# Attention and a mixture of experts in one kernel: where the leftover batch's first transposes stand in TensorE's order

## The chip, the cores and the metric

The kernel runs on one core of a Trainium2 chip. The core has TensorE (PE in the profile; its weight loads are listed as PEld), VectorE (DVE), ScalarE (ACT), GpSimd (POOL) and SyncE (SP), which issues DMA transfers, as GpSimd does too. The metric is the device time of one execution in microseconds (us), as the median of five runs.

## What is computed

Multi-query attention (8 batches, 16 heads, 384 tokens, head size 64, one key and value head) gives 3072 token vectors of 1024 values. Each token then chooses one of 4 groups and one of the group's 4 experts, and goes through that expert's two matrices:

```python
scores = scale * np.matmul(q, k.transpose(0, 1, 3, 2))
attn = softmax(scores)
x = np.matmul(attn, v)                # (batch, head, token, 64) -> (3072, 1024)
g_idx = np.argmax(x @ w_group, axis=1)
e_idx = np.argmax(xg @ w_expert[g], axis=1)
h = np.maximum(xg[mask_e] @ w1[g, e], 0.0)
ye = h @ w2[g, e]
out[tok_idx] = combined[:, None] * ye     # combined: product of the two gate weights
```

(`softmax` stands for the usual lines, and `xg` for the tokens of group `g`.)

## The kernel before

**Stages.** The loop over `p` (24 blocks of 128 tokens, three for each batch) does the attention. For each finished batch the kernel finds the expert that most of its tokens chose, loads that expert's two matrices and runs the whole batch through them. Tokens that chose another expert are rare: one pair of batch and expert is taken as the "leftover" and computed apart at the end of the kernel, for up to 32 tokens gathered from its batch. A general, slow branch (`rare_block`) stands behind that for all other cases.

**Units.** A batch's pass through its expert is cut into 14 units of PE work by `moe_units`: eight `h_unit`s (called h0 to h7 below), each of 8 matmuls (L407) into one PSUM tile `hps`, which ScalarE evicts into `hT` (L408); and six `y_unit`s (y00, y01, y10, y11, y20, y21: block of 128 tokens, half of the columns), each of 8 matmuls (L417) into `yps`, which ScalarE scales and evicts into a row tile `y` (L419); when both halves of a block are there, SP stores it (L447). `fill(n)` emits the next n units. The order of instructions on each engine is that of the program text; no scheduler moves them. So the calls of `fill` decide which PE work stands between the steps of a longer chain.

**PSUM.** All side results (`hps`, `yps`, `pb`, `px`, `ph` and others) take turns on one ring of three buffers (`ps_s`, tag "s"). A tile can be written only when the tile three places before it in the program's order has been read out.

**The end of the kernel**, in the order of the text, from the last block's attention on:

- `weigh(NP - 1)` (L656) finishes batch 7's tokens; GpSimd casts them to bf16 (L301), and SP writes them to DRAM as `x_bf` (L303).
- L659: SP reads the leftover batch's tokens, `xe`, back from `x_bf`. The batch is known only at run time, so this read waits for that write.
- `fill(2)`, the gates of batch 7, `fill(3)`, the ranks of the leftover's tokens (L675 to L689), `fill(1)`, `counts`, `fill(1)`, the matmuls `pg` (L697, L698). With these, batch 6's last units and h0 to h3 of batch 7 have run.
- L710: `fill(3)` emits h4, h5 and h6.
- L712 to L719: for each of the three token blocks, 8 transposes of `xe` on PE into one PSUM tile `pb` (L715; pb0, pb1, pb2 below), VectorE's copy to `xt` (L717), and `fill(1)`: h7 behind pb0, y00 behind pb1, y01 behind pb2.
- L723: 24 matmuls `px` gather the chosen tokens out of the three `xt`; VectorE copies them to `xc` (L725).
- Then the leftover's expert: `ph` (L732) with its first matrix, `phT` (L738), `py` (L746) with its second, and `yc` (L748), each with a unit behind it (y10, y11, y20). The second matrix is loaded by `leftover_w2` (L582), which `fill` calls when batch 6's last unit is out. GpSimd scatters `yc` into `out` (L750), `spread` (L458 to L469) adds it to batch 7's last block, and the last stores go out (L466, L445).

Of the kernel before, what the change touches and what calls it, by code (L numbers as in the profile page):

```python
# [21 lines left out]
def kernel(  # L22
# [53 lines left out]
    def side(shape, dtype, name):  # L76
        return ps_s.tile(shape, dtype, tag="s", name=name)
# [351 lines left out]
    def first_units(b):  # L429
        rows = {}  # L430

        def place(st, cs):
            if cs.start == 0:
                rows[st] = pool.tile([P, Dm], FP32, tag="y", bufs=3, name="y")
            return rows[st][:, cs]

        def closes(st):
            return b == B - 1 and st == ST - 1

        def store(st, cs, y):  # L440
            if closes(st):
                if cs.start == 0:
                    leftover["row"] = y
                else:
                    nc.sync.dma_start(out=outv[b, :, st, cs], in_=y)  # L445
            elif cs.stop == Dm:
                nc.sync.dma_start(out=outv[b, :, st, :], in_=rows[st][:])  # L447

        def merge(st, cs, ps, y):
            if not closes(st) or cs.start == 0:  # L450
                return False
            if cs.start == CW:
                spread()
            nc.vector.scalar_tensor_tensor(out=y, in0=ps[:], scalar=gsel[b][:, st:st + 1], in1=leftover["y"][:, cs.start - CW:cs.stop - CW], op0=OP.mult, op1=OP.add)
            return True
        return moe_units(wts[b][0], wts[b][1], xbf[b], lambda: gsel[b], place, store, merge, lambda st, nh: 2 if closes(st) and nh == 1 else 1)
# [26 lines left out]
    def fill(n):  # L483
        while n > 0:
            if not units:
                if begun[0] >= B or begun[0] not in wts:
                    return
                units.extend(first_units(begun[0]))
                begun[0] += 1
            units.pop(0)()  # L490
            n -= 1
            ran[0] += 1
            if ran[0] == (FO + 2 * ST) * (B - 2) + FO:
                leftover_w1()
            if ran[0] == (FO + 2 * ST) * (B - 1):
                leftover_w2()
# [77 lines left out]
    def leftover_w1():  # L574
        leftover["e"], leftover["b"] = parts_of(leftover["reg"])
        w1 = wpool.tile([P, KO, F], BF16, tag="w1", name="w1")
        load_w1(w1, leftover["e"])
        leftover["w1"] = w1

    def leftover_w2():  # L580
        w2 = wpool.tile([P, FO, Dm], BF16, tag="w2", name="w2")
        nc.gpsimd.dma_start(out=w2[:], in_=w2f[bass.ds(leftover["e"], 1)].rearrange("a p k f -> (a p) k f"))  # L582
        leftover["w2"] = w2
    for p in range(NP):
        b, st = divmod(p, ST)
# [121 lines left out]
    nc.vector.tensor_sub(out=small[:, 1:2], in0=nfl[:], in1=small[:, 0:1])  # L707
    nex = pool.tile([1, 1], I32, tag="nex", bufs=1, name="nex")
    nc.vector.tensor_copy(out=nex[:], in_=small[0:1, 1:2])
    fill(3)  # L710
    xtok = []
    for st in range(ST):  # L712
        pb = side([P, Dm], BF16, "pb")
        for ko in range(KO):
            nc.tensor.transpose(out=pb[:, ko * P:(ko + 1) * P], in_=xe[:, ko, st * P:(st + 1) * P], identity=ident_bf[:])  # L715
        xt = pool.tile([P, Dm], BF16, tag="pt", bufs=9, name="xt")
        nc.vector.tensor_copy(out=xt[:], in_=pb[:])  # L717
        xtok.append(xt)
        fill(1)  # L719
    px = side([P, KO, CAP], FP32, "px")  # L720
    for ko in range(KO):
        for st in range(ST):
# [183 lines left out]
```

## Time and profile before

| what | value |
|---|---|
| median of five runs | 461.11 us (460.64 to 461.69) |
| the profiled execution | 460.88 us |
| its span in the profile | 459.4 us |
| PE clock granted | 0.995 of full speed |
| matmuls of the attention's scores, L251 | 1152, 142.7 us |
| matmuls of the attention's values, L290 | 1152, 141.1 us |
| matmuls of the h units, L407 | 512 shown, 86.7 us |
| matmuls of the y units, L417 | 380 shown, 85.0 us |
| transposes of `xe`, L715, from the first to the last start | 435.4 to 439.7 us |
| read of `xe`, issue to landing | 7.2 us |

All views are of one execution. Times in them count from the start of the span. A row of a timeline gives the start, the busy time, the engine, the line, the operation with its output and input tiles, the number of instructions, and in brackets the engine's idle time before the group with what ended it. A matmul's duration includes its way through the array, in which the next matmul already runs; distances between starts tell what a group costs. Some records of matmuls are missing in a trace (7 of 8 shown in some groups).

### The profile page before, as it was taken

What the parts mean: (1) busy time and instruction counts of PE and PEld (TensorE: products, weight loads), DVE (VectorE), ACT (ScalarE), POOL (GpSimd) and SP (SyncE); (2) the same over time, 40 slices, a digit from 0 to 9 for tenths busy, and PEclk for the clock granted to TensorE, in tenths of its full rate; (3) what the DMA queues carried; (4) which work ended last, traced back from release to release, by engine and by line L of the source; (5) the groups of instructions that cost most, each with busy time, mean ns of one, the idle gap of its engine ahead of it and who ended that gap; (6) DMA issues with size and microseconds to landing.
All of it is one profiled execution on the core that took longest, in us unless ns stands there. A gap on an engine that the chain in (4) does not pass through costs nothing.

```text
span 459.4 us, 10188 instructions
## 1 busy us (share of the span) xinstructions
PE 448.7 (98%) x4196; PEld 199.8 (43%) x4208; DVE 308.3 (67%) x488; ACT 241.9 (53%) x345; POOL 60.4 (13%) x83
## 2 busy tenths in 40 slices
PE   8999999999999999999999999999999999999893
PEld 6343445333643345433553335433464335434552
DVE  3899965499717996099843997269960999674421
ACT  2966643676337753576346763376535764541331
POOL 1004003000120113000030001200130000500000
PEclk9999999999999999999999999999999999999998
DMA  8787997996699395992969747994859920799982
GB/s 159 94 147 111 217 213 114 258 201 140 106 182 254 70 189 96 232 227 74 172 97 262 147 117 126 170 257 79 171 98 228 235 70 17 117 211 236 275 220 105
DMA packets 152454, 74.55 MB, mean 162 GB/s; under 512 B 120256, under 2 KB 138944, under 8 KB 152400
## 3 DMA queue, kind: packets, MB, share of 16 engines
q0 software_dynamic: 28416, 37.81, 48.4%
q1 hardware_dynamic: 122656, 35.68, 33.3%
q8 instruction: 35, 0.57, 0.5%
q10 hardware_dynamic: 1328, 0.33, 0.4%
q14 instruction: 19, 0.16, 0.1%
HBM read 92.62 MB, written 19.01 MB: 243 GB/s over the span
## 4 chain that ended last, share of the span: by engine, by line
PE 90%; DMA 3%; issue 3%; DVE 1%; POOL 0%; ACT 0%; SPq 0%; POOLq 0%; ACTq 0%
PE s L251 28%; PE o L290 25%; PE hps L407 16%; PE yps L417 16%; PE gps L312 2%; DMA x_bf<-xbf 2%; DMA xe<-x_bf 2%; PE qps L228 1%; PE warm L152 1%; POOL xbf L301 0%; DVE presum L261 0%; PE sm L273 0%; PE pb L715 0%; DVE rinv L280 0%; DVE xT L300 0%
## 5 line engine op out<-in xcount | busy, mean ns | idle before, releaser
L253 ACT ACTIVATE pt<-s 128x1024 f32<-128x1024 f32 x144 | 142.1, 1026 | 72.4 <-PE s L251 71.6
L251 PE MATMUL s<-qT,kT 64*64 64x512 f32 x1152 | 142.7, 594 | 0.0
L290 PE MATMUL o<-pt,v 64*64 64x512 f32 x1152 | 141.1, 590 | 0.0
L261 DVE TENSOR_TENSOR presum<-presum,pt 128x1024 f32<-128x1024 f32 x96 | 116.6, 1215 | 15.2 <-ACT pt L253 9.8
L407 PE MATMUL hps<-xbf,w 128*128 128x384 bf16 x512 | 86.7, 326 | 0.0
L417 PE MATMUL yps<-w,hT 128*128 128x512 bf16 (+1 forms) x380 | 85.0, 375 | 0.6
L259 DVE TENSOR_TENSOR presum<-pt 128x1024 f32<-128x1024 f32 x24 | 29.4, 1223 | 76.8 <-ACT pt L253 75.4
L290 PEld LDWEIGHTS o<-pt,v 64*64 64x64 f32 x1152 | 43.4, 133 | 76.8 <-issue 73.0
L251 PEld LDWEIGHTS s<-qT,kT 64*64 64x64 f32 x1152 | 40.8, 133 | 66.8 <-issue 60.2
L301 POOL CAST xbf<-xT 128x1024 bf16<-128x1024 f32 x24 | 25.0, 1041 | 302.9 <-DVE xT L300 302.9
L407 PEld LDWEIGHTS <-w 128*128 128x128 bf16 x512 | 48.1, 98 | 37.6 <-issue 6.5
L419 ACT ACTIVATE y<-yps,gsel 128x512 f32<-128x512 f32 x47 | 32.3, 687 | 58.8 <-PE yps L417 57.2
L408 ACT ACTIVATE hT<-hps 128x384 bf16<-128x384 f32 x64 | 31.2, 488 | 52.1 <-PE hps L407 48.0
L417 PEld LDWEIGHTS <-hT 128*128 128x128 bf16 x392 | 37.5, 98 | 44.2 <-issue 2.4
L145 POOL DMA_DIRECT2D w<-in_moe_w_dram x36 | 24.8, 707 | 58.1 <-DVE gsel L395 45.0
L300 DVE TENSOR_TENSOR xT<-o,rinv 128x1024 f32<-128x1024 f32 x24 | 29.1, 1214 | 2.5 <-PE o L290 2.5
L280 DVE STREAM_TRANSPOSE rinv<-rc 128x1024 f32<-128x1024 f32 x24 | 29.9, 1246 | 0.8
L265 DVE TRANSPOSE_TENSOR_REDUCE fold<-presum 128x32 f32<-128x1024 f32 x24 | 29.6, 1231 | 0.0
L243 DVE STREAM_TRANSPOSE qT<-qraw 128x1024 f32<-128x1024 f32 x20 | 23.6, 1202 | 0.0
L209 ACT ACTIVATE qraw<-qraw 128x1024 f32<-128x1024 f32 x21 | 22.0, 1048 | 0.0
L273 PEld LDWEIGHTS sm<-fold,sel 64*64 64x64 f32 x192 | 7.3, 133 | 13.3 <-issue 13.3
L371 ACT ACTIVATE ex<-dl 128x60 f32<-128x60 f32 x8 | 2.0, 253 | 20.1 <-DVE dl L369 20.1
(152 smaller groups left out, 161.9 us busy)
## 6 DMA issues: line engine op xcount, KB each, us to landing
w<-in_moe_w_dram POOLq DMA_DIRECT2D x36, 512.0 KB, 11.4
w<-in_moe_w_dram POOLq DMA_DIRECT2D x9, 2048.0 KB, 26.0
out_dram<-y SPq DMA_DIRECT2D x23, 512.0 KB, 7.3
qraw<-in_q_dram SPq DMA_DIRECT2D x56, 192.0 KB, 3.7
x_bf<-xbf SPq DMA_DIRECT2D x8, 768.0 KB, 3.9
v<-in_v_dram SPq DMA_DIRECT2D x16, 96.0 KB, 3.2
k<-in_k_dram SPq DMA_DIRECT2D x28, 48.0 KB, 2.6
qn<-in_q_dram SPq DMA_DIRECT2D x4, 256.0 KB, 5.2
```

Of the source, the lines that this page charges most:

```text
L251: nc.tensor.matmul(out=ps[64 * c:64 * c + 64, a, :], lhsT=kT[b][r, j * D:(j + 1) * D], rhs=qT[p][r, c * CW:(c + 1) * CW], start=True, stop ...
L253: nc.scalar.activation(out=t[:], in_=ps[:], func=ACTF.Exp, scale=scale)
L259: nc.vector.tensor_add(out=presum[p][:], in0=pt[p, 0][:], in1=pt[p, 1][:])
L261: nc.vector.tensor_add(out=presum[p][:], in0=presum[p][:], in1=pt[p, j][:])
L265: nc.vector.tensor_reduce(out=fold[p][:], in_=presum[p][:].rearrange("p a (n i) -> p (a n) i", i=32), axis=AX, op=OP.add, apply_transpose= ...
L280: nc.vector.transpose(out=t[:].rearrange("p (b i) -> p b i", i=32), in_=rc[:].rearrange("p c b -> p (c b)").unsqueeze(2).to_broadcast([P, ...
L290: nc.tensor.matmul(out=o_ps[p][64 * a:64 * a + 64, c, :], lhsT=v_sb[b][r, j, :], rhs=pt[p, j][r, a, :], start=(j == 0), stop=(j == KB - 1))
L300: nc.vector.tensor_mul(out=xT[b][:, :, ts], in0=o_ps[p][:].rearrange("p c (h n) -> p (c h) n", n=P), in1=rinv[p][:].rearrange("p (h n) -> ...
L407: nc.tensor.matmul(out=ps[:, 0:S], lhsT=w1[:, ko, fc * P:(fc + 1) * P], rhs=xb[:, ko, :], start=(ko == 0), stop=(ko == KO - 1))
L408: nc.scalar.activation(out=state["h"][:, fc, :], in_=ps[:, 0:S], func=ACTF.Relu)
L417: nc.tensor.matmul(out=ps[:], lhsT=state["h"][:, fo, st * P:(st + 1) * P], rhs=w2[:, fo, cs], start=(fo == 0), stop=(fo == FO - 1))
L419: nc.scalar.activation(out=y, in_=ps[:], func=ACTF.Copy, scale=gs_of()[:, st:st + 1])
```

## The change

```diff
     nc.vector.tensor_copy(out=nex[:], in_=small[0:1, 1:2])
-    fill(3)
+    fill(4)
     xtok = []
     for st in range(ST):
         pb = side([P, Dm], BF16, "pb")
...
         xt = pool.tile([P, Dm], BF16, tag="pt", bufs=9, name="xt")
         nc.vector.tensor_copy(out=xt[:], in_=pb[:])
         xtok.append(xt)
-        fill(1)
+        if st > 0:
+            fill(1)
```

`fill(4)` now emits h4 to h7 ahead of the first transposes, and no unit follows pb0. PE's order around it goes from h6, pb0, h7, pb1, y00, pb2, y01, px to h6, h7, pb0, pb1, y00, pb2, y01, px. The ring of three PSUM buffers is taken in the same new order. The other engines keep their order, and every instruction is still there.

## The prediction

> **What bounds the kernel now.** I read the page first: which engine is full, and what the chain of work that ended last is made of.
>
> ```profile
> span 459.4 us, 10188 instructions
> PE 448.7 (98%) x4196; PEld 199.8 (43%) x4208; DVE 308.3 (67%) x488; ACT 241.9 (53%) x345; POOL 60.4 (13%) x83
> ...
> PE 90%; DMA 3%; issue 3%; DVE 1%; POOL 0%; ACT 0%; SPq 0%; POOLq 0%; ACTq 0%
> ```
>
> TensorE (PE) is busy 98% of the span and makes 90% of the chain; DMA makes 3%, so there is little to win except where PE stands still. Next I read the chain in order of time from 420 us on, where the diff lies:
>
> ```profile
> 420.33 7.66 DMA x_bf<-xbf
> ...
> 428.11 7.21 DMA xe<-x_bf
> 435.32 0.05 issue
> 435.37 0.62 PE pb L715 x8
> 435.99 1.30 PE hps L407 x8
> 437.29 0.45 PE pb L715 x8
> ```
>
> Columns: start, duration, what. The chain leaves PE here: batch 7's tokens are written to DRAM (7.66 us), the leftover batch's tokens are read back from it (7.21 us, landing at 435.32), and only then do the first transposes start. From there to the end the chain is PE. What PE did meanwhile is in its timeline (start, busy, what, idle before it):
>
> ```profile
> 432.72 1.46 PE L407 MATMUL hps<-xbf,w 128*128 128x384 bf16 x8
> 435.37 0.62 PE L715 MATMUL pb<-ident_bf,xe 128*128 128x128 bf16 x8 [1.19 <-DMA xe<-x_bf]
> 435.83 1.46 PE L407 MATMUL hps<-xbf,w 128*128 128x384 bf16 x8
> 437.13 0.61 PE L715 MATMUL pb<-ident_bf,xe 128*128 128x128 bf16 x8
> 437.57 1.89 PE L417 MATMUL yps<-w,hT 128*128 128x512 bf16 x7
> 439.30 0.61 PE L715 MATMUL pb<-ident_bf,xe 128*128 128x128 bf16 x8
> 439.75 1.89 PE L417 MATMUL yps<-w,hT 128*128 128x512 bf16 x8
> 441.47 0.76 PE L723 MATMUL px<-pick_bf,xt 128*128 128x32 bf16 x24
> ```
>
> PE ends hidden unit h6 (the seventh) at 434.18 and stands still for 1.19 us until xe lands, although the next unit in its order, h7, needs nothing of xe. No other PE gap of this size stands between 430 us and the end. The x7 is a missing record; the unit has 8 matmuls.
>
> **The change part by part.** The count of instructions is the same on every engine; h7 (8 matmuls of L407) moves ahead of the first transposes pb0, and pb0 and pb1 become neighbours. I work with start-to-start distances from the timeline, since a group's busy time includes the tail of its last matmul under the next group: pb0 435.83 - 435.37 = 0.46, h7 437.13 - 435.83 = 1.30, pb1 0.44, unit y00 1.73, pb2 0.45, y01 1.72. From pb0's start to px's start: 441.47 - 435.37 = 6.10 us.
>
> h7 in the hole: h6 started at 432.72; at 1.30 a unit, h7 starts at 434.02 and the next group could start at 435.32. The half of the weights that holds its columns was already needed by h4, and its PSUM buffer is the one h4 used, evicted by ScalarE at about 432. So h7 costs nothing: the wait for xe hides 1.19 of it, and the 0.11 of start-up overlap that the wait exposed hides the rest. If xe were there early, this cover would be gone and the move would be worth nothing.
>
> pb0: still the later of PE free (435.32) and xe there, started at 435.37 as before. Nothing that the xe transfer shares a queue with is moved ahead of 435 us, so I keep its landing at 435.32.
>
> After pb0: pb1, y00, pb2, y01, px without h7 between: px starts at 435.37 + 6.10 - 1.30 = 440.17 instead of 441.47. **Sum: 1.30 us less**, if no new wait appears. The waits to check, by the order in PSUM's three side buffers (A, B, C; h7 now takes A, pb0 B, pb1 C, y00 A, pb2 B, y01 C, px A):
>
> y00 at 435.37 + 0.46 + 0.44 = 436.27 needs A empty, that is h7 evicted. h7's last matmul ends at 434.02 + 1.46 = 435.48; the eviction follows the matmuls by 0.04 and takes 0.49 (old order: matmuls end 437.29, eviction 437.33):
>
> ```profile
> 437.33 0.49 ACT L408 ACTIVATE hT<-hps 128x384 bf16<-128x384 f32 x1 [2.61 <-PE hps L407]
> 437.77 0.69 DVE L717 COPY xt<-pb 128x1024 bf16<-128x1024 bf16 x1 [1.05 <-PE pb L715]
> ```
>
> So A is free at 436.01, 0.26 ahead of y00. That is the thinnest margin. This wait is new: before, A held pb0, and h7's result was only needed by y00's last matmul. Bounds: 0 to, if the eviction started one whole eviction (0.49) late, 0.23; I take 0, as ScalarE has nothing else queued there. Behind y00 on PE everything would shift by it.
>
> pb2 at 438.00 needs pb0's copy: 0.66 after pb0's start as now, 436.03 to 436.72; pb1's copy runs behind it on VectorE to about 437.4, and y01 (438.45) needs that. px needs y00's eviction (0.69, ending near 438.8 against 440.17) and pb2's copy (0.69 from 438.65, to 439.34). None waits.
>
> DMAs that come earlier with PE: the row store of batch 7's first block (SP, L447) is issued when y01 is evicted, now 442.39, then 441.09; the second block's, now 447.53, by 1.30 too, and the scatter on GpSimd and the last stores behind it likewise. On SP's queue nothing stands ahead of them that is late: xe was issued at 428.11 and the two stores of batch 6 at 428.58. The first store shares the DMA engines with the load of the leftover expert's second weights (L582), issued at 425.11:
>
> ```profile
> w<-in_moe_w_dram POOLq DMA_DIRECT2D x1, 2048.0 KB, 20.9
> ...
> 441.00:441.50 0.50, 0.50 (x4) 0.22 (x3) 0.00 (x0) 0.00 (x0) 0.00 (x0) 1.00 1.12 221
> 444.00:444.50 0.50, 0.50 (x24) 0.49 (x24) 0.00 (x0) 0.45 (x1) 0.00 (x0) 1.00 1.04 328
> ```
>
> It lands at 425.11 + 20.9 = 446.0. Its first reader, py (L746), starts at 448.55 now and would at 447.25: 2.55 us of slack become 1.25. The two window rows (last column GB/s) show the engines full in both, but 221 GB/s with the load nearly alone and 328 with the store beside it. The store, issued 1.30 earlier, can push the load by at most what it takes ahead of it. Lowest bound 0, as both now overlap anyway; highest by a row of the same size below, under the rivals. I take a landing short of 447.25, so 0.
>
> By the Trainium skill (DMA: Bandwidth & Descriptors, "Queues, rings and completion order") each DMA engine takes packets in turn from every queue that has work, which speaks against an earlier store. With half the turns lost for 1.30 us the load would come 0.65 us later, an estimate from that page's rule, at 446.65; the sum would stay at 1.30. The rows' rise from 221 to 328 GB/s says that even this is too much.
>
> After px nothing changes in order, so all of it shifts: xc's copy, y10, ph (its weights landed at 398.98 + 32.3 = 431.3), py, the spread, the last stores and the 6.3 us from the last VectorE instruction (453.11) to the span's end.
>
> **The sum against the clock.** The profiled execution took 460.88 us (span 459.4, the rest lies around it). 460.88 - 1.30 = 459.58. The median of the five runs, 461.11, is 0.23 above that execution, so **459.8** as a median. A measurement of this kernel can tell about 0.2%, 0.92 us, from no change: faster means under 460.19, slower over 462.03.
>
> **The rivals.**
> A, forecast: h7 fills the wait, 459.8. For it: an exposed 1.19 us with its releaser named, and work beside it that needs nothing. Its gain cannot exceed h7's 1.30; a wait shorter by d makes it smaller by about d. Own range 459.4 to 460.2.
> B, the wait in timed executions is shorter than in this one: x_bf and xe, 7.66 and 7.21 us, go through busy engines, while seven earlier x_bf writes were quicker (all eight have a median of 3.9, and the one near 380 us took 3.4). Against it: the profiled execution is within 0.23 of the median, and the engines are as busy there every time. With 0.6 us less wait the gain is 0.7: 460.4.
> C, slower: the second weights become the wait in front of py. Place: PE's first matmul of L746, with y20 and all the rest queued behind it. It decides from a landing at 447.25 on, and the kernel is slower than before once it is past 448.55, that is 23.4 us after issue instead of 20.9. For it: the nine loads of this size have a median of 26.0 us. At 26.0 it lands at 451.1, py waits 3.85, and the net is 2.55 slower: 463.7. Against it: those nine ran beside other weight loads, and the store's bytes only change places in the last 5 us of this one.
> D, the change does not do quite what it says: y00 is held by h7's eviction in buffer A, or the two transposes in a row run into VectorE's copies. Price 0.23 from the bound above, up to 0.5 with a whole eviction: gain 0.8 to 1.07, 460.0 to 460.3.
>
> **How the numbers follow.** A 0.72, B 0.12, C 0.10, D 0.06. The time is A's, 459.8. Range 459.3 to 461.2: A with 0.5 below it for the scatter of the runs (0.47 from lowest to median), up over D and B to a shade above no gain; C lies outside. Faster by over 0.2%: A and part of D, 0.75. Within: B, the other part of D and the light end of C, 0.16. Slower: C, 0.09.
>
> **What would show it.** Right: no PE idle of note before pb0 (under 0.3 us); hps in front of it starting near 434.0; pb0 near 435.4 and pb1 0.46 behind; px near 440.2; py near 447.25 without a DMA releaser; the span near 458.1. Wrong: a wait named by xe in front of pb0 still near 1 us (xe moved later too), a wait of y00 on ScalarE, a wait of py on the weight load, or a px that starts near 441.5 after all.

## The result and the profile after

| | before | changed |
|---|---|---|
| median | 460.96 us (43 runs) | 459.60 us (22 runs) |
| ratio to before | | 0.9972, 95% interval 0.9967 to 0.9978 |
| span of the profiled execution | 459.4 us | 458.2 us |

The ratio is a gain of 1.29 us (1.0 to 1.5). The page of the changed kernel, the lines that stood first before:

```profile
span 458.2 us, 10188 instructions
PE 448.6 (98%) x4196; PEld 199.8 (44%) x4208; DVE 308.2 (67%) x488; ACT 242.0 (53%) x345; POOL 60.5 (13%) x83
...
PE 87%; DMA 6%; issue 4%; DVE 1%; ACT 0%; POOL 0%; ACTq 0%; POOLq 0%
```

PE's busy time is the same within 0.1 us; the span is 1.2 us shorter. So idle time went, not work. The DMA share of the chain rose from 3 to 6%, which says that another transfer is now in it. The timeline of PE in the changed kernel (start, busy, what; idle before it in brackets):

```profile
430.15 5.36 PE L407 MATMUL hps<-xbf,w 128*128 128x384 bf16 x32
435.35 1.06 PE L715 MATMUL pb<-ident_bf,xe 128*128 128x128 bf16 x16
436.24 1.89 PE L417 MATMUL yps<-w,hT 128*128 128x512 bf16 x7
...
440.14 0.75 PE L724 MATMUL px<-pick_bf,xt 128*128 128x32 bf16 x24
...
447.50 1.06 PE L747 MATMUL py<-w,hc 128*32 128x256 bf16 x32 [0.21 <-DMA w<-in_moe_w_dram]
```

h4 to h7 now run in one piece (32 matmuls), pb0 and pb1 follow (16), and there is no idle time before pb0: the 1.19 us named by `xe` are gone. px starts at 440.14 instead of 441.47, so 1.33 us earlier. py, however, starts only 1.05 us earlier (447.50 instead of 448.55): a small wait for the leftover expert's second weights has appeared. The chain of the changed kernel shows the same from the other end:

```profile
425.13 22.23 DMA w<-in_moe_w_dram
447.37 0.14 issue
447.50 1.06 PE py L747 x32
448.56 0.98 PE yps L417 x8
```

That load landed 20.9 us after its issue before, and 22.2 us after it now.

### The profile page after: what moved, and what is told of

Its sections match the earlier page's. It is cut to its first block, busy times and chain, and to the rows that moved or that the text cites. A ratio compares the mean times of both kernels' runs of the same rounds, so it can differ in the third digit from the quotient of the medians.

```text
span 458.2 us, 10188 instructions
## 1 busy us (share of the span) xinstructions
PE 448.6 (98%) x4196; PEld 199.8 (44%) x4208; DVE 308.2 (67%) x488; ACT 242.0 (53%) x345; POOL 60.5 (13%) x83
## 4 chain that ended last, share of the span: by engine, by line
PE 87%; DMA 6%; issue 4%; DVE 1%; ACT 0%; POOL 0%; ACTq 0%; POOLq 0%
PE s L251 28%; PE o L290 25%; PE hps L407 16%; PE yps L417 14%; DMA w<-in_moe_w_dram 5%; PE gps L312 2%; DMA qn<-in_q_dram 1%; PE qps L228 1%; DVE presum L261 0%; PE sm L273 0%; DVE rinv L280 0%; DVE xT L300 0%; POOL xbf L301 0%; ACT pt L253 0%; PE py L747 0%
```

## The experiments

The origin of a trace moves by some tenths of a microsecond from one execution to the next. So the table measures inside the stage: from the first matmul of h4, which no kernel here moves, to the first of py. "PE idle before pb0" is the idle time that PE's rows show, "load" is the second weights' time from issue to landing, "h4 to py" the stage; all times are in us. Counted from h4, px came 1.36 us earlier in the changed kernel and py 1.08.

| kernel | ratio to before (95%) | PE idle before pb0 | load | h4 to py |
|---|---|---|---|---|
| before | 1 | 1.19 | 20.9 | 18.43 |
| changed | 0.9972 (0.9967 to 0.9978) | none | 22.2 | 17.35 |
| changed, again | 0.9972 (0.9962 to 0.9983) | none | 22.0 | 17.11 |
| y00 between pb0 and pb1 | 0.9977 (0.9967 to 0.9987) | none | 22.1 | 17.23 |
| adjacent only | 1.0001 (0.9992 to 1.0010) | 1.23 | 20.8 | 18.47 |
| two units ahead | 0.9979 (0.9970 to 0.9988) | none | 22.0 | 17.16 |
| one unit less | 1.0037 (1.0023 to 1.0050) | 2.53 | 20.8 | 21.45 |
| before, no second load | 0.9977 (0.9968 to 0.9986) | none | none | 17.07 |
| changed, no second load | 0.9976 (0.9966 to 0.9986) | none | none | 17.07 |
| second load in halves | 0.9977 (0.9966 to 0.9988) | none | 16.3 and 21.0 | 17.07 |
| store held back | 1.0002 (0.9993 to 1.0011) | none | 20.7 | 17.07 |

17.07 us is what the stage takes when PE waits for nothing, in either order. The kernel before stands 1.36 us above it, more than the 1.19 us of its idle row: from h4's start to pb0's start it takes 5.25 us (435.37 - 430.12), and three units take 3.90, so the standstill is 1.35 us from start to start, the last 0.16 us of h6's busy time included. The small rests in other rows are waits too, seen in the distances between PE's starts: 0.28 us of py in the changed kernel; 0.10 us of y01 and 0.06 us of py with y00 between; 0.09 us of the third block's transposes with two units ahead; 0.03 us of pb0 in the changed kernel run again. In the last, `xe` landed at 435.46 and pb0 started at 435.51: one unit covers the wait, but with nothing to spare.

**Which part of the edit is worth the time.** First the changed kernel without the standing together of pb0 and pb1 (h7 stays ahead):

```diff
-        if st > 0:
+        if st != 1:
             fill(1)
```

> The changed kernel with y00 put between pb0 and pb1 again and nothing between pb1 and pb2: h6, h7, pb0, y00, pb1, pb2, y01, px. Theory (h7 ahead of pb0 fills the wait for xe): the gain stays whole, ratio to the kernel before 0.997, about 459.6 us, PE idle before pb0 under 0.2 us. Rival (the gain comes from two transposes standing together, or from what stands between them): a good part of the 1.3 us is lost, ratio 0.9985 or more.

Then the standing together alone, with h7 behind it:

```diff
-    fill(4)
+    fill(3)
...
         if st > 0:
-            fill(1)
+            fill(3 - st)
```

> Only the standing together: h6, pb0, pb1, h7, y00, pb2, y01, px; nothing is moved ahead of pb0. Theory (the wait for xe): PE idles 1.2 us before pb0 as in the kernel before, ratio 1.000 within 0.0007, about 460.9 us. Rival (adjacency): the gain of the changed kernel, ratio 0.997.

The first keeps the gain (0.9977), the second has none (1.0001). PE's timeline of the second:

```profile
430.22 4.06 PE L407 MATMUL hps<-xbf,w 128*128 128x384 bf16 x24
435.51 1.07 PE L715 MATMUL pb<-ident_bf,xe 128*128 128x128 bf16 x16 [1.23 <-DMA xe<-x_bf]
```

Both transposes stand together here and the idle time is back, with the same releaser. Adjacency is worth nothing that these runs can tell; the unit ahead of pb0 is worth all of it.

**Is it the wait, or is each unit further back worth something?** One unit more ahead of the transposes than in the changed kernel:

```diff
-    fill(4)
+    fill(5)
...
-        if st > 0:
+        if st > 1:
             fill(1)
```

> One unit more ahead of the transposes: h6, h7, y00, pb0, pb1, pb2, y01, px. Theory (the gain is capped by the wait, which one unit already covers): same as the changed kernel within 0.2 us, about 459.6 us, xe there 1.7 us before pb0 wants it. Rival (each unit moved ahead is worth its own 1.3 to 1.7 us): 458 us.

0.9979 (0.9970 to 0.9988): the interval overlaps the changed kernel's (0.9967 to 0.9978) and shows no further gain. Once the wait is covered, another unit ahead brings nothing. Then the other direction, from the kernel before:

```diff
-    fill(3)
+    fill(2)
...
         xtok.append(xt)
-        fill(1)
+        fill(2 if st == 0 else 1)
```

> The kernel before with the edit turned round: h6 too is taken from in front of the transposes, so the order is h5, pb0, h6, h7, pb1, y00, pb2, y01, px. Theory (PE waits for xe with whatever is not in front of pb0): the wait before pb0 grows by one unit, from 1.2 to 2.5 us, and the kernel is 1.3 us slower than the kernel before, 462.3 us, ratio 1.0028. Rival (the work behind pb0 makes up for it, or xe comes earlier with it): ratio 1.000 to 1.001.

The wait is as expected, the time is not: 463.19 us against 461.31, 1.7 us slower by the ratio instead of 1.3, and the stage took 3.02 us more than before. PE's timeline, then four stretches of the windows view (time, length, busy time of PE, PEld, DVE, ACT and POOL, each with its instructions, then granted clock, DMA share, GB/s):

```profile
435.74 0.71 PE L715 MATMUL pb<-ident_bf,xe 128*128 128x128 bf16 x8 [2.53 <-DMA xe<-x_bf]
436.25 4.39 PE L407 MATMUL hps<-xbf,w 128*128 128x384 bf16 x16
440.48 0.61 PE L715 MATMUL pb<-ident_bf,xe 128*128 128x128 bf16 x8
```

```profile
435.00:436.00 1.00, 0.26 (x5) 0.26 (x6) 0.00 (x0) 0.00 (x0) 0.00 (x0) 1.00 1.12 297
436.00:436.50 0.50, 0.50 (x8) 0.40 (x6) 0.01 (x1) 0.00 (x0) 0.00 (x0) 0.64 1.03 283
436.50:437.00 0.50, 0.50 (x3) 0.26 (x2) 0.50 (x1) 0.00 (x0) 0.00 (x0) 0.50 1.03 307
...
439.50:440.00 0.50, 0.50 (x5) 0.30 (x4) 0.00 (x0) 0.04 (x1) 0.00 (x0) 0.95 1.15 332
```

The wait grew from 1.19 to 2.53 us, by about the 1.30 of a unit. But behind it h6 and h7 took 4.23 us from start to start instead of 2.60, because the granted clock stood at 0.50 from about 436.1 to 439.5 us. The six timed executions fall into two groups: 462.1 to 462.7 us with a mean clock of 0.997, and 463.7 to 464.1 us with 0.994; the profiled one belongs to the second. The first group is 0.8 to 1.4 us above the median before, about the price of the wait alone. That the other two executions of the second group lost the clock at this place is inferred from their times, 1.0 us and more above the first group; only one of the six has a profile. The mean clock alone would not show it: it also counts the half clock behind the last matmul (from 454.9 us to the end in the traces before and changed), and the changed kernel run again has 0.994 in an execution of 460.03 us.

**The same wait removed by another way.** If the order matters only because `xe` is late, an early `xe` must make the two orders equal. The load of the second weights shares the DMA engines with `xe`; both kernels were run without it:

```diff
     def leftover_w2():
-        w2 = wpool.tile([P, FO, Dm], BF16, tag="w2", name="w2")
-        nc.gpsimd.dma_start(out=w2[:], in_=w2f[bass.ds(leftover["e"], 1)].rearrange("a p k f -> (a p) k f"))
-        leftover["w2"] = w2
+        leftover["w2"] = wts[B - 1][1]
```

> The kernel before with the same load left out and py reading batch 7's second weights instead. Theory (the whole gain is the exposed wait for xe): xe lands at 434.3 us or earlier, PE's wait before pb0 falls from 1.2 us to 0.2 us or less, and the kernel comes within 0.3 us of the changed kernel without that load, about 459.6 us, though its order is the old one. Rival (the order is worth 1.3 us by itself): 461.0 us, 1.3 us or more behind the changed kernel without that load.

> The changed kernel without the load of the leftover expert's second weights: py reads batch 7's second weights instead, with as many matmuls, and the leftover tokens' rows are another product. Theory: xe lands earlier, since the load no longer shares the DMA engines with it; h7 covers the rest, and py no longer waits: about 0.25 us less than the changed kernel, 459.35 us.

In the old order `xe` landed 5.7 us after its issue instead of 7.2 (6.2 in the new order), and its timeline has no idle time before pb0:

```profile
430.57 4.06 PE L407 MATMUL hps<-xbf,w 128*128 128x384 bf16 x24
434.47 0.61 PE L713 MATMUL pb<-ident_bf,xe 128*128 128x128 bf16 x8
434.92 1.46 PE L407 MATMUL hps<-xbf,w 128*128 128x384 bf16 x8
```

Here pb0 follows h6 after 3 x 1.30 us, h7 stands behind it as it always did, and the stage takes 17.07 us, to the hundredth what the new order takes without the load. The ratios are 0.9977 and 0.9976. So the order is worth nothing by itself; it is worth the exposed wait. One expectation failed: the changed kernel without the load was to be 0.25 us faster than with it, and is not measurably so (459.83 us; intervals overlap). The stage did get shorter (17.07 against 17.35 us), but from the end of the last VectorE instruction to the end of the span the executions of the table take between 6.0 and 6.4 us (the held store's apart), and a quarter of a microsecond drowns in that.

**The new wait of py.** Does the store of batch 7's first block, now issued 1.3 us earlier, slow the second load? In one kernel it was held back behind the second block's store:

```diff
             elif cs.stop == Dm:
-                nc.sync.dma_start(out=outv[b, :, st, :], in_=rows[st][:])
+                if b == B - 1 and st == 0:
+                    return
+                for s in ([1, 0] if b == B - 1 else [st]):
+                    nc.sync.dma_start(out=outv[b, :, s, :], in_=rows[s][:])
```

> The changed kernel with the store of batch 7's first block issued only behind that of the second block (about 446.2 us instead of 441.1 us). Theory (the store, issued 1.3 us earlier, slowed the load of the second leftover weights, 22.2 us instead of 20.9 us, so that py waits from 447.2 to 447.5 us): without it the load lands at 446 us or before, py has no DMA releaser, span about 0.25 us shorter, ratio 0.9966 against 0.9972. Rival (the load's landing wanders by itself by a microsecond): py still waits for it, ratio 0.9972.

The load landed after 20.7 us and py did not wait (17.07 us). Yet the kernel lost all it had gained. The chain says where:

```profile
446.85 0.33 SPq L450
447.19 0.04 issue
447.23 5.58 DMA out_dram<-y
452.81 0.03 POOLq L754
...
454.05 1.00 POOL out_dram L754
```

The scatter's row in the changed kernel, and with the store held back:

```profile
449.95 1.09 POOL L751 DMA_INDIRECT out_dram<-yc,rows  x1 [23.94 <-ACT yc L749]
```

```profile
453.95 1.09 POOL L754 DMA_INDIRECT out_dram<-yc,rows  x1 [27.29 <-DMA out_dram<-y]
```

GpSimd's scatter into `out` waits for the stores to `out` that were issued before it: in all eleven traces it starts 1.14 to 1.15 us after the later of batch 7's two full-row stores has landed, in the changed kernel too (448.81), although its row names `yc` there. The held store lands at 452.8, and the scatter starts at 453.95, which is 23.15 us behind h4 instead of 19.80 (449.95 - 430.15 in the changed kernel); it had been off the chain, and now ends it. In the other direction the load was cut in two, so that the first half of py needs only the first MB:

```diff
-        nc.gpsimd.dma_start(out=w2[:], in_=w2f[bass.ds(leftover["e"], 1)].rearrange("a p k f -> (a p) k f"))
+        for c in range(2):
+            k = slice(c * FO // 2, (c + 1) * FO // 2)
+            nc.gpsimd.dma_start(out=w2[:, k], in_=w2f[bass.ds(leftover["e"], 1), :, k].rearrange("a p k f -> (a p) k f"))
```

> The changed kernel with the load of the leftover expert's second weights as two transfers of 1 MB, so that py's first 16 matmuls need the first one only. Theory (py waits for the end of the load): the first half is there long before 447 us, py starts at 447.2 us, and its second half waits 0 to 0.1 us at most: 0.2 us less than the changed kernel, 459.4 us. Rival (two issues cost as much as they save, or the second half lands later than the whole did): 459.6 us or more.

py's wait is gone here too (17.07 us), and the time, 459.81 us beside 460.95 before, cannot be told from the changed kernel's. Last, the changed kernel once more:

> The changed kernel once more, unaltered, beside the run with one unit less. Theory: ratio 0.9972 within its interval, PE without a wait for xe, and py waiting for the second weights by 0 to 0.4 us, as the load's landing wanders (22.2 us after issue in the first trace, 22.0 and 22.1 us in two runs with y00 between or ahead). Rival (the first trace's wait of py was a chance of one execution): py starts 11.9 us behind pb0 without a wait, the load lands 21 us after its issue.

```profile
435.51 1.07 PE L715 MATMUL pb<-ident_bf,xe 128*128 128x128 bf16 x16
...
447.39 1.06 PE L747 MATMUL py<-w,hc 128*32 128x256 bf16 x32
```

py starts 11.88 us behind pb0, without a releaser: no wait, although the load took 22.0 us. Both halves of the question have an answer. The slower load is no chance: it goes with the time at which the store is issued. In the four executions that issue the store 15.9 to 16.0 us after the load (changed twice, y00 between, two units ahead) the load took 22.0 to 22.2 us; where the store comes 17.3 us after it (before, adjacent only), 20.8 and 20.9; at 20.3 us (one unit less) 20.8, and at 21.1 us (held back, in the changed order) 20.7. Whether py feels it is a matter of 0.1 us: 0.28 us of the stage with a load of 22.2 us, 0.06 us with 22.1 (y00 between), nothing in the two executions with 22.0.

The store's data, however, did not move earlier. In the DMA packets of the two traces, sorted by queue, the 512 KB of the store of batch 7's first block begin at 443.71 us before (issued at 442.39) and at 443.62 us in the changed kernel (issued at 441.06), and land at 447.27 and 447.53 us. Nor does the bulk of the load come later: 19.5 us after its issue 30 and 32 KB of it are left. Only this rest takes longer, with the last packet at 445.67 us before and 447.03 us in the changed kernel.

## Why the prediction was right

- **The sum.** 1.30 us was forecast, 1.29 measured; 459.8 us forecast, 459.60 measured, of which 0.15 is that the median before came out lower with more runs (460.96 instead of 461.11). That the two gains agree to a hundredth is luck: the interval is 1.0 to 1.5 us, and the stage gained 1.08 us in the first profiled execution and 1.32 in the second.
- **h7 costs nothing in the hole.** Shown: PE has no idle time before pb0, and px came 1.33 us earlier (1.36 counted from h4). That the hole, not the place, is what counts is shown by two units ahead (no more gain), by adjacency alone (none) and by the old order with an early `xe` (the same 17.07 us).
- **xe's landing unmoved.** 7.3 us after issue against 7.2; pb0 started at 435.35 (435.37 forecast).
- **y00 and buffer A.** The thinnest margin named held: h7's eviction ended at 435.55 + 0.49 = 436.04, 0.2 us ahead of y00 at 436.24. No wait of y00, pb2, y01 or px is in the two traces of the changed kernel.

```profile
435.55 0.49 ACT L408 ACTIVATE hT<-hps 128x384 bf16<-128x384 f32 x1 [0.81 <-PE hps L407]
```

- **The load of the second weights** is where a term was mis-sized. The landing was put at 446.0 us, or 446.65 by the estimate from the Trainium skill (DMA: Bandwidth & Descriptors, "Queues, rings and completion order", which has the engines take turns between queues), with 447.25 as the point from which py waits. It measured 447.37 (22.23 us after its issue at 425.13), and py started at 447.50 with a DMA releaser, which the prediction had named as a sign of being wrong; it cost 0.28 us in that execution and nothing in the second. The load took 1.1 to 1.4 us longer with the store issued 1.3 us earlier, not half of that and not nothing: the GB/s rows that were read as spare room said nothing of when the last piece of the load would land. The 1.3 us of shared turns that the estimate counted with are not in the packets, since the store's data began to move at the same time as before. Nor was SP's queue free of anything late: batch 6's second store, issued at 429.05, landed only at 441.94. Why the last pieces of the load come later, is not settled. Rival C had the right place and stayed at its threshold; its 26.0 us did not occur.
- **Rival B** (a shorter wait in the timed executions) is out: its gain of 0.7 us lies below the interval of 1.0 to 1.5.
- **Rival D** had two mechanisms, and neither was seen in the changed kernel. A wait of its kind, PE held by an eviction on ScalarE, stands in two variants: with y00 between, y01 starts at 438.85, just behind the end of y00's eviction at 438.80, and with two units ahead pb2 starts at 438.96 behind 438.91. It cost 0.10 and 0.09 us.

## What to carry to other kernels

An engine that stands still for a transfer is helped by whatever ready work can be put in front of the waiting instruction, up to the length of the wait and no further: one unit of 1.30 us against 1.35 us of standstill from start to start took nearly all of it, and a second brought nothing. Everything behind the wait then comes earlier, its DMAs too, so look for the loads that are still under way there: issuing one store 1.3 us earlier made the load beside it land 1.1 to 1.4 us later, in its last few KB. That is one load and one store, and no rule for others. Before holding a store back, look for who waits for it: here it was the scatter, 3.4 us later.

## What the runs showed of the hardware

A gap in PE's work may cost more than its length. After 2.53 us without a matmul the granted clock stood at 0.50 for about 3.4 us, and two units took 4.23 us instead of 2.60; by their times (463.7 to 464.1 us against 462.1 to 462.7) half of that kernel's six executions probably paid it. After gaps of 1.19 and 1.23 us the clock stayed at 1.00 in the traces. The Trainium skill (TensorE: Matmul & The Clock Gate, "What's actually happening") gives a free-running window of about 3.4 us and has the clock fall after an idle one; the length of the slow stretch here is near that, but the gap before it was shorter than a window.

The clock records of the traces say more. Every stretch of full clock in the eleven traces is a whole multiple of 3.413 us (450.56, 447.15, 430.08 and 20.48 us), and the slow stretch between the last two, from 436.13 to 439.55 us, is one such step. If the clock is decided at the end of each step, as these lengths suggest, the step that ended with the fall began at 432.72 us, and PE idled for 2.53 us of it (433.21 to 435.74). With adjacency alone the step from 432.25 to 435.66 us, counted back from that trace's fall at 456.14, holds the whole gap of 1.23 us, and the clock stayed. So the share of a step that must be idle lies, by this working, between 1.23 and 2.53 of 3.41 us; where a gap falls among the steps would then decide whether it costs anything more. That last point is not shown here.

The same 2 MB load took 20.7 to 20.9 us when a 512 KB store on another queue was issued 17.3 us or more after it, and 22.0 to 22.2 us when the store came after 16.0 us: a step between two points 1.3 us apart, with no change from 17.3 to 21.1. In all six executions with an issue at 15.9 to 17.3 us the store's first packet moved 18.5 to 18.6 us after the load's issue, so up to 2.6 us after its own; without the load it moved 0.83 us after its own issue.
